# Moving the gate's small tiles to the left side of on-chip memory: all large tiles shift by a fraction of 512 bytes

## The chip, the core and the metric

The kernel runs on one core of a Trainium2 chip. The metric is the device time of one execution in microseconds. Before the change it is 1930.12 us, the median of three runs (1930.12, 1932.39, 1927.75).

## The reference

Three stages follow one another, all in float32:

```python
k_p, v_p = k and v averaged over 8 neighbouring positions
attn = softmax(q @ k_p.T / 8) @ v_p                  # 4 batches, 8 heads, 576 positions
x = attn as [2304, 512]
h = x @ w_in ; x = (h * cos(h)) @ w_out              # 512 -> 2048 -> 512
P = exp(x @ w_gate - max) ; 8 rounds of row and column normalization
out = sum over 8 experts e of P[:, e] * (relu(x @ w1[e]) @ w2[e])   # 512 -> 1024 -> 512
```

The experts are two thirds of the span: each expert's two weight matrices are used in two units of 512 hidden columns, 16 units in all, against three pairs of token blocks (a pair is 768 tokens). That is 48 steps.

## The kernel before, in words

Every float32 operand of a product is split into a high and a low part, and a product is three TensorE matmuls (high by high, high by low, low by high). Each product of a step is computed by Strassen's scheme: seven products of half-size blocks, named P1 to P7.

**One step.** The first layer (`first_layer`, L1057, matmuls on L1077) has the weights `whi`/`wlo` as the stationary operand and the tokens `xc` as the moving operand of 384 columns: 84 matmuls. ScalarE and VectorE apply relu, combine the blocks and split them into `gh`/`gl` (`strassen_result`, L1380). The second layer (`strassen_layer`, L1449, matmuls on L1457) has `gh`/`gl` as the stationary operand and the weights `vhi`/`vlo` as the moving operand of 256 columns: 126 matmuls. In the order of the instructions first-layer matmuls of one step alternate with second-layer matmuls of the step before. The weights come in as `raw` tiles by DMA and are cut into parts by ScalarE, VectorE and GpSimd (`w1_pieces`, L1252, `w2_pieces`, L1288). Tokens are loaded again for every step (`x_loaded`, L1360).

**What sets the order.** The program is a list of nodes (`add`, L169), each with an engine, an estimated duration and the tiles it touches. `schedule` (L263) walks the list with these estimates and writes out each engine's instructions in a fixed order. It asks `place` (L240) whether a tile's slot is free and whether the slot's group is open. It knows slots by name and never by address.

**Where tiles lie.** On-chip memory has a stack on the left, which grows upwards, and one on the right, which grows downwards. Tiles belong to kinds, kinds to pools, pools to groups (L439 to L448). `Group.open` (L88) puts the pools of a group on its stack, one after the other, in the order in which they were named. `base`, `first`, `second` and later `more` are on the left; `early`, then `mid`, `ahead`, `turn` and `late` are on the right. `mid` and what follows it may open when no tile of `early` has any user left. L98 to L100 put a tile `edge` that nothing writes or reads ahead of the pools of `early` and of `mid`; it takes 64 bytes of a partition.

**The addresses.** They follow from the sizes, here in bytes of a partition, and what matters below is what is left of them past a multiple of 512. The left stack starts with a scratch area of 2048, four constants (128), `warm` (64) and `ident` (512): 2752, which is 192 past a multiple of 512. The tokens' slots `xp` (6144 each), the first layer's weights `wp` (2048) and the accumulators (6144) are multiples of 512, so all of them lie at 192. Then come the gate's `wgr` (512), `sel` (64) and `lg` (576). They end 128 further, so whatever follows on the left lies at 320: the raw weights `rawp`, the split activations `gph`/`gpl` and `gbh`/`gbl` (tiles `gh` and `gl`), the second stage's `xq`, `wq`, `tp`, and the accumulators `acx`. The right stack starts at a multiple of 512. Of `early`, the 64 bytes of `edge` put the conversion tiles `cvm`, `cvw`, `cvs` at 448. Of `mid`, `edge` (64), `ones` (512), `pr` (576) and the six scratch tiles `sk` of the gate's normalization (256) make 1408, so that the second layer's weights `wp2` (tiles `vhi` and `vlo`) and all that follow on the right (`xt`, `tmp`, `cps`, `cpc`, `cpt`) lie at 128.

The gate's tiles are made at L1184 to L1190 and used by `logits` (L1195) and `normalization` (L1213). Of `sel` only the first 8 columns are ever used.

Of the kernel before, what the change touches and what calls it, by code (L numbers as in the profile page):

```python
# [23 lines left out]
P = 128  # L24
T = B * S
DM = H * D
KC = DM // P
FU = 512
FC = FU // P
E = 8  # L30
# [3 lines left out]
NT = T // P  # L34
# [6 lines left out]
GW = 32  # L41
# [36 lines left out]
class Group:  # L78
# [9 lines left out]
    def open(self):  # L88
        if self.stack is not None:
            return  # L90
        if self.over:
            self.over.open()
        for g in self.after:
            if not g.closed and g.stack is not None:
                g.stack.close()
            g.closed = True
        self.stack = self.graph.ctx.enter_context(ExitStack())
        if self.name in ("early", "mid"):  # L98
            edge = self.stack.enter_context(self.graph.tc.tile_pool(name="edge" + self.name, bufs=1, side=self.side))
            edge.tile([P, 8], F32, name="edge" + self.name)  # L100
        for pool in self.pools:
            self.pools[pool] = self.stack.enter_context(
                self.graph.tc.tile_pool(name=pool, bufs=1, side=self.side, reuse_waits="tile"))
# [40 lines left out]
class Graph:  # L144
# [18 lines left out]
    def buf(self, kind, shape, dtype, name):  # L163
        return Buf(kind, shape, dtype, name)
# [268 lines left out]
def fused_kernel(ctx: ExitStack, tc: tile.TileContext, qT, kT, vT, v0, k1, v1, wa1, wb1, wa2, wb2, wg, out):  # L433
    nc = tc.nc
    g = Graph(ctx, tc)
# [3 lines left out]
    base = g.group("base")  # L439
    first = g.group("first")  # L440
    second = g.group("second")
    early = g.group("early", "right")
    mid = g.group("mid", "right", (early,))
# [10 lines left out]
    def many(group, pool_name, n, strict=False):  # L454
        return g.kind(group, pool_name, [str(i) for i in range(n)], strict)
# [20 lines left out]
    k_pt = many(early, "ptp", 1)  # L476
    k_ck = {n: g.kind(early, "ck", [n]) for n in ("band", "minus", "kbd0", "kbd1")}
    k_gc = {n: g.kind(mid if n in ("ones", "pr") else base, "gc" + n, [n]) for n in ("ones", "wgr", "sel", "lg", "pr")}
    k_sk = {n: g.kind(mid, "sk", [n]) for n in ("m1", "m2", "nm", "rw", "cs", "cr")}
    k_w2 = many(ahead, "wp2", W2, True)  # L480
    k_wd = g.join(k_cs, k_m, k_cw, strict=True)
    k_wu = g.kind(ahead, "wp2", [str(i) for i in range(10)], True)
# [682 lines left out]
    for u in range(U1):  # L1165
# [16 lines left out]


    gate = {n: buf(k_gc[n], s, F32, n) for n, s in (  # L1184
        ("ones", [P, P]), ("wgr", [P, KC, GW]), ("sel", [P, 2 * E]), ("lg", [P, NT, E]), ("pr", [P, NT, E]))}
    ones, wgr, sel, lg, pr = (gate[n] for n in ("ones", "wgr", "sel", "lg", "pr"))
    add("V", 0.17, lambda: nc.vector.memset(ones.tile, 1.0), [], [ones])
    load(lambda: wgr.tile, lambda: wg, P * KC * GW * 4, writes=[wgr])
# [397 lines left out]
```

## Time and profile before

| | |
|---|---|
| median of three runs | 1930.12 us (1927.75 to 1932.39) |
| the profiled execution's own time | 1929.34 us |
| its span, from the first to the last instruction | 1927.6 us |
| mean granted TensorE clock | 0.999 |
| TensorE, matmuls | 1907.3 us busy, 99% of the span, 13012 matmuls |
| VectorE, ScalarE, GpSimd | 1531.9, 1096.6, 427.4 us busy |
| DMA | 406.79 MB, 211 GB/s over the span |

The profiled execution is 0.8 us under the median. Its own time is 1.7 us longer than its span. A matmul's listed duration overlaps with its neighbours', so the pace of TensorE is read from the starts of matmuls that follow one another, or from the pieces of the chain of waits, which give the time of a row of them.

### The profile page before, as it was taken

The page shows a single profiled execution, that of the slowest core. Times are in us where ns is not written, and L with a number is a line of the kernel's source. Part 1 is how long each engine was busy: PE and PEld are TensorE (multiplying, and loading weights), DVE is VectorE, ACT ScalarE, POOL GpSimd, SP SyncE. Part 2 cuts the span into 40 slices and gives each one's busy share as a digit, 9 for nine tenths or more (in the row PEclk, how much of TensorE's full clock was granted, in tenths as well). Part 3 has the DMA queues.
Part 4 walks back from the last instruction along what each step waited for, and adds up shares of the span by engine and source line. Part 5 has one row for each costly group of instructions (what it writes and reads, how often), then busy time and mean ns, then how long its engine had stood idle before and what let it go on. Part 6 is the DMA issues. An engine that isn't in the chain of part 4 may idle for free.

```text
span 1927.6 us, 34292 instructions
## 1 busy us (share of the span) xinstructions
PE 1907.3 (99%) x13012; PEld 1872.0 (97%) x13012; DVE 1531.9 (79%) x2823; ACT 1096.6 (57%) x2354; POOL 427.4 (22%) x341
## 2 busy tenths in 40 slices
PE   8999999999999999999999999999999999999999
PEld 6789998899999999999999999999999999999998
DVE  8998888987787777777787787777777877877776
ACT  5664445675556666555556565565555565655553
POOL 2523245453202021212112021212121120212120
PEclk9999999999999999999999999999999999999999
DMA  8567564487656546546546455465465464554552
GB/s 294 169 193 236 194 198 138 176 288 239 231 225 229 228 186 237 212 181 236 211 177 262 168 231 229 184 238 210 183 236 211 178 262 170 229 231 180 229 216 113
DMA packets 107478, 406.79 MB, mean 211 GB/s; under 512 B 11825, under 2 KB 16561, under 8 KB 107313
## 3 DMA queue, kind: packets, MB, share of 16 engines
q1 hardware_dynamic: 106768, 403.55, 56.4%
q8 instruction: 102, 1.67, 0.4%
q0 software_dynamic: 544, 1.05, 0.3%
q14 instruction: 64, 0.52, 0.1%
HBM read 363.40 MB, written 41.16 MB: 210 GB/s over the span
## 4 chain that ended last, share of the span: by engine, by line
PE 91%; DVE 5%; ACT 1%; DMA 1%; issue 1%; POOL 0%; SPq 0%; DVEq 0%; POOLq 0%; ACTq 0%
PE pc L1457 21%; PE py L1077 17%; PE qc L1457 16%; PE pv L1077 11%; PE px L1077 11%; PE po L894 3%; PE po L895 3%; PE po L896 3%; PE ph L894 1%; PE ph L896 1%; PE ph L895 1%; PE ptr L803 0%; DVE at L540 0%; DVE cw L858 0%; PE psc L714 0%
## 5 line engine op out<-in xcount | busy, mean ns | idle before, releaser
L1457 PE MATMUL pc<-vhi,gl 128*128 128x256 f32 x1152 | 321.6, 279 | 0.0
L1457 PE MATMUL pc<-vhi,gh 128*128 128x256 f32 x1152 | 321.5, 279 | 0.0
L1457 PE MATMUL pc<-vlo,gh 128*128 128x256 f32 x1152 | 321.3, 279 | 0.0
L1077 PE MATMUL py<-xc,whi 128*128 128x384 f32 x1152 | 293.3, 335 | 0.0
L540 POOL TENSOR_TENSOR raw<-raw 128x512 f32<-128x512 f32 x45 | 59.1, 1314 | 895.4 <-DVE wlo L540 542.1
L540 DVE TENSOR_TENSOR gl<-sf,gh 128x384 fp32r<-128x384 f32 x384 | 228.4, 624 | 30.9 <-ACT gh L523 30.9
L523 ACT ACTIVATE gh<-sf 128x384 fp32r<-128x384 f32 x384 | 195.0, 524 | 92.1 <-DVE sf L540 90.1
L1457 PE MATMUL qc<-vhi,gh 128*128 128x256 f32 x864 | 243.6, 282 | 0.9 <-DVE qc L540 0.5
L1457 PE MATMUL qc<-vhi,gl 128*128 128x256 f32 x864 | 241.6, 280 | 0.0
L1457 PE MATMUL qc<-vlo,gh 128*128 128x256 f32 x864 | 240.8, 279 | 0.0
L1457 PEld LDWEIGHTS pc<-vlo,gh 128*128 128x128 f32 x1152 | 216.6, 188 | 0.0
L1457 PEld LDWEIGHTS pc<-vhi,gl 128*128 128x128 f32 x1152 | 216.3, 188 | 0.0
L1457 PEld LDWEIGHTS pc<-vhi,gh 128*128 128x128 f32 x1152 | 215.5, 187 | 0.1
L1077 PEld LDWEIGHTS py<-xc,whi 128*128 128x128 f32 x1152 | 199.7, 188 | 1.3 <-ACT py L523 0.6
L1077 PE MATMUL px<-xc,whi 128*128 128x384 f32 x768 | 195.8, 335 | 0.0
L1077 PE MATMUL pv<-xc,whi 128*128 128x384 f32 x768 | 195.8, 335 | 0.0
L1077 PE MATMUL py<-xc,wlo 128*128 128x384 f32 x576 | 193.2, 335 | 0.0
L1457 PEld LDWEIGHTS qc<-vhi,gh 128*128 128x128 f32 x864 | 161.8, 187 | 3.4 <-DVE qc L540 1.1
L1457 PEld LDWEIGHTS qc<-vlo,gh 128*128 128x128 f32 x864 | 162.5, 188 | 0.0
L1457 PEld LDWEIGHTS qc<-vhi,gl 128*128 128x128 f32 x864 | 162.3, 188 | 0.0
L1077 PEld LDWEIGHTS pv<-xc,whi 128*128 128x128 f32 x768 | 130.7, 188 | 0.0
L1077 PEld LDWEIGHTS px<-xc,whi 128*128 128x128 f32 x768 | 130.5, 188 | 0.0
(235 smaller groups left out, 4676.1 us busy)
## 6 DMA issues: line engine op xcount, KB each, us to landing
xc<-xc SPq DMA_DIRECT2D x357, 768.0 KB, 6.7
wc<-wac SPq DMA_DIRECT2D x112, 256.0 KB, 3.3
raw<-wa SPq DMA_DIRECT2D x48, 512.0 KB, 4.0
raw<-wb SPq DMA_DIRECT2D x48, 512.0 KB, 7.4
wac<-wc SPq DMA_DIRECT2D x64, 256.0 KB, 3.8
out<-acc SPq DMA_DIRECT2D x18, 256.0 KB, 2.0
qc<-qt SPq DMA_DIRECT2D x30, 128.0 KB, 3.1
wf<-cw SPq DMA_DIRECT2D x12, 256.0 KB, 3.6
```

The lines of the kernel that those rows point to most:

```text
L523: lambda: nc.scalar.activation(out=out(), in_=in_(), func=func, **{k: v() if callable(v) else v for k, v in more.items()}),
L540: (nc.gpsimd if e == "G" else nc.vector).tensor_tensor(out=out(), in0=in0(), in1=in1(), op=op)
L894: nc.tensor.matmul(out=ps, lhsT=lh, rhs=rh, start=(i == 0), stop=False)
L895: nc.tensor.matmul(out=ps, lhsT=lh, rhs=rl, start=False, stop=False)
L896: nc.tensor.matmul(out=ps, lhsT=ll, rhs=rh, start=False, stop=(i == total - 1))
L1077: nc.tensor.matmul(out=ps(), lhsT=l[:, k], rhs=r[:, c, :], start=(start and c + n == 0), stop=(c + n == 3), skip_group_check=True)
L1457: nc.tensor.matmul(out=ps, lhsT=l[:, r], rhs=m[:, k], start=(start and h + n == 0), stop=(h + n == 3), skip_group_check=True)
```

## The change

Three edits, all of them about where tiles lie. `early` has no `edge` tile any more. The six scratch tiles `sk` move from `mid` on the right to `base` on the left. `sel` is declared with 48 columns in place of 16; its use stays the same.

```diff
@@ Group.open
-        if self.name in ("early", "mid"):
+        if self.name == "mid":
             edge = self.stack.enter_context(self.graph.tc.tile_pool(name="edge" + self.name, bufs=1, side=self.side))
             edge.tile([P, 8], F32, name="edge" + self.name)
@@ fused_kernel
-    k_sk = {n: g.kind(mid, "sk", [n]) for n in ("m1", "m2", "nm", "rw", "cs", "cr")}
+    k_sk = {n: g.kind(base, "sk", [n]) for n in ("m1", "m2", "nm", "rw", "cs", "cr")}
@@ fused_kernel, the gate
-        ("ones", [P, P]), ("wgr", [P, KC, GW]), ("sel", [P, 2 * E]), ("lg", [P, NT, E]), ("pr", [P, NT, E]))}
+        ("ones", [P, P]), ("wgr", [P, KC, GW]), ("sel", [P, 6 * E]), ("lg", [P, NT, E]), ("pr", [P, NT, E]))}
```

By the same sums: on the left `wgr`, `sel`, `lg` and `sk` now take 512 + 192 + 576 + 256 = 1536 bytes, three times 512, so what follows lies at 192 and no longer at 320. On the right `edge`, `ones` and `pr` take 1152, so `wp2` and what follows lie at 384 and no longer at 128. The tiles of `early` move up by 64 bytes, `cvm`, `cvw` and `cvs` to a multiple of 512. Tiles of `xp`, `wp` and the first four accumulators stay where they are.

## Rows read from the trace of the kernel before

**Rows 1.** The page, part 1: busy us, share, instructions of each engine.

```profile
PE 1907.3 (99%) x13012; PEld 1872.0 (97%) x13012; DVE 1531.9 (79%) x2823; ACT 1096.6 (57%) x2354; POOL 427.4 (22%) x341
```

**Rows 2.** Stretches of the span: length, each engine's busy us, clock, DMA share, GB/s.

```profile
0.00:100.00 100.00, 90.07 (x554) 73.21 (x555) 89.79 (x176) 62.30 (x133) 40.94 (x51) 1.00 0.73 235
100.00:200.00 100.00, 98.39 (x569) 94.35 (x568) 89.32 (x168) 56.23 (x110) 28.75 (x24) 1.00 0.66 212
200.00:300.00 100.00, 98.56 (x566) 98.35 (x565) 86.44 (x152) 49.63 (x100) 41.31 (x39) 1.00 0.65 207
300.00:400.00 100.00, 97.62 (x618) 88.52 (x617) 86.14 (x149) 61.13 (x110) 44.43 (x35) 1.00 0.46 158
400.00:500.00 100.00, 100.00 (x573) 100.00 (x572) 73.32 (x123) 56.01 (x111) 42.10 (x27) 1.00 0.69 240
500.00:600.00 100.00, 99.61 (x691) 96.55 (x690) 85.45 (x196) 65.14 (x136) 12.00 (x7) 1.00 0.63 242
600.00:1900.00 1300.00, 1300.00 (x9272) 1298.31 (x9271) 1004.53 (x1832) 737.09 (x1634) 217.90 (x159) 1.00 0.55 212
```

**Rows 3.** The chain of waits, 1000 to 1012 us: start, us, what.

```profile
1000.75 1.04 PE py L1077 x6
1001.79 0.70 PE qc L1457 x6
1002.50 2.12 PE pc L1457 x18
1004.61 1.04 PE pv L1077 x6
1005.66 0.70 PE qc L1457 x6
1006.36 0.71 PE pc L1457 x6
```

**Rows 4.** The page, part 5: the two layers' largest groups of matmuls.

```profile
L1457 PE MATMUL pc<-vhi,gl 128*128 128x256 f32 x1152 | 321.6, 279 | 0.0
...
L1077 PE MATMUL py<-xc,whi 128*128 128x384 f32 x1152 | 293.3, 335 | 0.0
...
L1457 PE MATMUL qc<-vhi,gh 128*128 128x256 f32 x864 | 243.6, 282 | 0.9 <-DVE qc L540 0.5
```

**Rows 5.** The chain of waits, 400 to 500 us.

```profile
400.14 2.08 PE py L1077 x12
...
406.95 1.05 PE pv L1077 x6
...
410.62 1.06 PE pv L1077 x6
...
415.90 1.04 PE py L1077 x6
```

**Rows 6.** Instructions in order of time, TensorE, 465.1 to 467.2 us.

```profile
465.10 0.34 PE L894 MATMUL po<-gh,wc 128*128 128x384 f32 x1
...
466.15 0.34 PE L894 MATMUL po<-gw,wc 128*128 128x384 f32 x1
...
467.20 0.34 PE L1077 MATMUL px<-xh,wc 128*128 128x384 f32 x1
```

**Rows 7.** Groups by line, ScalarE, 384 elements: busy us, mean ns, idle before.

```profile
L523 ACT ACTIVATE gh<-spare 128x384 fp32r<-128x384 f32 x96 | 50.1, 522 | 38.1 <-DVE spare L1407 38.0
L523 ACT ACTIVATE gh<-c 128x384 fp32r<-128x384 f32 x96 | 49.8, 519 | 1.5
...
L523 ACT ACTIVATE gh<-r 128x384 fp32r<-128x384 f32 x80 | 39.8, 518 | 22.5 <-PE po L896 11.2 <-DVE r L540 11.1
...
L523 ACT ACTIVATE gw<-r 128x384 fp32r<-128x384 f32 x16 | 8.2, 519 | 1.1 <-DVE r L540 1.1
```

**Rows 8.** Groups by line, VectorE, 512 elements.

```profile
L540 DVE TENSOR_TENSOR wlo<-raw,whi 128x512 fp32r<-128x512 f32 x79 | 53.9, 698 | 14.2 <-ACT whi L523 14.2
...
L540 DVE TENSOR_TENSOR vlo<-raw,vhi 128x512 fp32r<-128x512 f32 x68 | 46.4, 683 | 31.2 <-ACT vhi L523 31.2
```

**Rows 9.** The page, part 6: DMA issues, KB each, us to landing.

```profile
xc<-xc SPq DMA_DIRECT2D x357, 768.0 KB, 6.7
...
raw<-wa SPq DMA_DIRECT2D x48, 512.0 KB, 4.0
raw<-wb SPq DMA_DIRECT2D x48, 512.0 KB, 7.4
```

## The prediction

> **What bounds the kernel now.** I read the busy shares first, then the stretches of the span, then the chain of waits, and last the durations of single groups. The shares name TensorE: 1907.3 of 1927.6 us [rows 1]. A share is an average, so the stretches come next. They show two different parts. Up to 600 us TensorE's busy time falls short of the stretch by 9.93, 1.61, 1.44, 2.38, 0 and 0.39 us, 15.75 us in all, and there attention, weight conversion and DMA share the work. From 600 to 1900 us it is busy 1300.00 of 1300 us while VectorE has 1004.53, ScalarE 737.09 and GpSimd 217.90, all at a granted clock of 1.00 of the 2.4 GHz level [rows 2]. The reader is to see that in these two thirds of the span nothing but TensorE's own pace counts: an operation that gets 10% slower on VectorE, or a load that lands a microsecond later, has room.
>
> The chain of waits gives that pace, because here it consists of matmuls alone. Eighteen second-layer matmuls take 2.12 us, 117.8 ns each; six first-layer matmuls take 1.04 us, 173.3 ns each [rows 3]. A step has 84 in the first layer and 126 in the second, 14.56 + 14.84 = 29.4 us, and 48 steps make 1411 us. So what the kernel does in the experts is 4032 intervals of 173.3 ns and 6048 of 117.8 ns. (The 6048 are 3 x 1152 and 3 x 864, one row of each shown [rows 4].)
>
> **The change part by part.** The three edits add no instruction and remove none: the `edge` tile is never touched, the extra columns of `sel` are never read or written, and `sk` holds the same tiles under the same names. Nothing is moved in any queue, SP's and GpSimd's included. The order of the work is also the same as far as I can follow it by hand: the planner asks only whether a slot is free and its group open. `sk` in `base` is open from the start, where in `mid` it had to wait for `early` to close; but its first user needs all six blocks' logits, which need the last output of the stage before, long after `early` has no users left. So the first part of the sum is **0 us for instructions and order**.
>
> Waits: tiles of `sk` used to lie on memory that the conversion tile `cvm` had held; that wait goes, on work of the stage before, whose output the gate's logits need anyway, 0 us. The tiles of `ahead`, `turn` and `late` now move by 256 bytes against `early`'s 64, and all left tiles by the same 384, so which new tile lies on which old one hardly changes: going through the sizes I find no overlap that is new between `early` and the weights `wp2`, and `wp2`'s third slot no longer touches a tile of `at`. 0 us.
>
> What is left is whether an address alone changes a duration. I take the engines one by one.
>
> *ScalarE.* The same copy of 384 elements takes 522 ns from an input at 192, 519 ns from one at 128 and 518 ns from one at 320, all into a tile at 320, and 519 ns into one at 192 [rows 7]. Four placements, 4 ns apart. 0 us.
>
> *VectorE.* The subtraction with its output and one input at 192 has a mean of 698 ns, that with both at 128 has 683 [rows 8]. The 15 ns may be placement or GpSimd at work beside it. For `vlo`, which moves from 128 to 384, I bound it by 0 and +15 ns: some 112 such operations on either engine, 1.7 us of VectorE time in a stretch where it is idle for 295 us. What covers it is that idle time; without the cover 1.7 us would show. 0 us.
>
> *DMA.* The `raw` loads, 96 of 512 KB, land after 4.0 and 7.4 us [rows 9] in tiles that go from 320 to 192; the token loads `xc` stay where they were. A tenth more on the slower ones would be 0.7 us each, and TensorE waits for none of them after 600 us [rows 2]. 0 us there. Before 600 us the waits are 15.75 us in sum; if a tenth of these hung on placement it would be 1.6 us either way. I keep that as an end, and take 0.
>
> *TensorE.* This is the term that decides. The first layer keeps both addresses (192 and 192): 0 us. The second layer's stationary operand goes from 320 to 192 and its moving operand from 128 to 384. No row has that combination, so I bound it. In the stretch from 400 to 500 us operands lie at 192, 320 and others in many combinations. Twelve matmuls of 384 columns take 2.08 us, and six take 1.04, 1.05 or 1.06 us [rows 5]; in the experts, with everything at 192, six take 1.04 us [rows 3]. The nearest row for the question is a pair side by side: the six matmuls from 465.10 us have a moving operand at 320 (`gh` and `gl`), the six from 466.15 us one at 192 (`gw`), and both sixes take 1.05 us [rows 6]. That says that moving an operand by 128 bytes is worth less than 0.01 us in six, or 2 ns each.
>
> The lower end: if the second layer ran at the first layer's pace per column, 173.3 x 256 / 384 = 115.6 ns, it would gain 2.2 ns on each of 6048, **-13 us**. The upper end: if it lost what the slowest six in the mixed stretch lose against the fastest, 1.06 against 1.04 us or 1.9%, it would take 120.1 ns, 2.3 ns more on each of 6048, **+14 us**. Between them I take 0, by the pair, which is the nearest row.
>
> The Trainium skill has a rule that would make of this much more. Its page "TensorE: Matmul & The Clock Gate", section "Back-to-back issue gap", gives 262 cycles for a warm matmul of 256 columns, 109.2 ns. By that the second layer carries 8.6 ns per matmul that the page does not know, and if placement were their cause and the change ended it, the sum would be an estimated -52 us. The same page, "Step-by-step: what each phase is for", says that stationary and moving operand come through two independent read ports, so that loading one does not slow the other; by that placement cannot be the cause. The trace bears out the second: the excess is there in every placement that it shows.
>
> **The sum.** 0 in each term, against the profiled execution's own time of 1929.34 us, which is 0.8 us under the median of the runs shown. I forecast the median, 1930.1 us.
>
> **The rivals.** *Faster: the old pair of addresses costs the second layer something.* Its excess over a bare 256 columns at 2.4 GHz (106.7 ns) is 11.1 ns, 10.4%; the first layer's over 160 ns is 13.3 ns, 8.3%. So the second layer is the slower of the two per column, and it is the one with operands on two different remainders. If the new pair takes it to the first layer's pace, the time is 1930.1 - 13 = 1917 us; with half of that 1923.5. Against it: a matmul has a fixed part as well as a part per column, and a fixed part weighs more on 256 columns than on 384 whatever the addresses are. Chance 0.25.
>
> *Slower: the new pair of addresses collides where the old one did not.* The place is the same 6048 matmuls, as the weight load of the next one runs while the moving operand streams. It decides from 0.65 ns per matmul on (3.9 us over 6048). With the full price above the time is 1930.1 + 14 = 1944 us. For it speaks that six matmuls in the mixed stretch can take 1.06 us; against it, that the same kind of six (`pv`) takes 1.06 us at one time and 1.05 at another in that stretch, so that its spread need not be one of placement, and that the pair at 465 us shows none. Chance 0.17.
>
> *The waits before 600 us shift.* The conversion tiles and the raw inputs move too, and with them the order in which VectorE and GpSimd meet. It is worth up to 1.6 us by the bound above, 1928.5 to 1931.7, and stays inside no change.
>
> *The change doesn't do what it says.* If a size were rounded otherwise than I take it, all large tiles would lie on some other remainder. By the rows that is the same question with the same two ends, so it has no chance of its own.
>
> **How the numbers follow.** A measurement of this kernel can tell about 0.2% from no change, 3.9 us. No change has the rest, 0.58, and its own range is 1926 to 1934. The 8-in-10 range takes in the half price of the faster case and stops short of its full price, and takes the nearer part of the slower case: 1918 to 1937. That leaves about 0.1 out on either side.
>
> **What would show it.** Right: second-layer pieces of eighteen at 2.12 us, first-layer pieces of six at 1.04 us, TensorE busy for all of 600 to 1900 us, and the same number of matmuls there to within a few. Faster, for the reason given: eighteen in 2.08 us, with the first layer unchanged, and some 85 matmuls more (0.9%) between 600 and 1900 us. Slower: eighteen in 2.16 us. I would be wrong in kind if the first layer's pace changed, whose operands did not move, or if the difference lay before 600 us.

## The result: 1908.0 us in the first runs, 1905.4 in a second set, 21 to 25 us less

The changed kernel takes 1908.03 us, the median of four runs (1904.94 to 1910.66), against 1929.34 (median of four, 1927.75 to 1932.39) for the kernel before: ratio 0.9887, 95% interval 0.9866 to 0.9908. A second set, run i2 below, gives 1905.43 against 1930.62: ratio 0.9870, 0.9855 to 0.9885. The prediction of no change was wrong; the change is faster, by 1.1 to 1.3%, and by more than the forecast range of 1918 to 1937 us allowed.

### The profile page after: what moved, and what is told of

Its sections match the earlier page's. It is cut to its first block, busy times and chain, and to the rows that moved or that the text cites. A ratio compares the mean times of both kernels' runs of the same rounds, so it can differ in the third digit from the quotient of the medians.

```text
span 1909.0 us, 34292 instructions
## 1 busy us (share of the span) xinstructions
PE 1889.6 (99%) x13012; PEld 1851.5 (97%) x13012; DVE 1530.6 (80%) x2823; ACT 1095.1 (57%) x2354; POOL 430.7 (23%) x341
## 3 DMA queue, kind: packets, MB, share of 16 engines
q0 software_dynamic: 544, 1.05, 0.3%
## 4 chain that ended last, share of the span: by engine, by line
PE 92%; DVE 6%; ACT 1%; issue 1%; DMA 1%; SPq 0%; DVEq 0%; ACTq 0%
PE pc L1457 20%; PE py L1077 17%; PE qc L1457 16%; PE px L1077 11%; PE pv L1077 11%; PE po L894 3%; PE po L896 3%; PE po L895 3%; PE ph L894 2%; PE ph L896 2%; PE ph L895 2%; DVE at L540 1%; PE ptr L803 1%; PE px L817 1%; PE psc L714 0%
## 5 line engine op out<-in xcount | busy, mean ns | idle before, releaser
L1457 PE MATMUL pc<-vlo,gh 128*128 128x256 f32 x1152 | 318.0, 276 | 0.0
L1457 PE MATMUL pc<-vhi,gl 128*128 128x256 f32 x1152 | 318.0, 276 | 0.0
L1457 PE MATMUL pc<-vhi,gh 128*128 128x256 f32 x1152 | 318.0, 276 | 0.0
L1457 PE MATMUL qc<-vhi,gh 128*128 128x256 f32 x864 | 241.6, 280 | 1.0 <-DVE qc L540 0.5
L1457 PE MATMUL qc<-vlo,gh 128*128 128x256 f32 x864 | 238.9, 276 | 0.0
L1457 PE MATMUL qc<-vhi,gl 128*128 128x256 f32 x864 | 238.8, 276 | 0.0
L1457 PEld LDWEIGHTS pc<-vhi,gh 128*128 128x128 f32 x1152 | 216.3, 188 | 0.1
L1457 PEld LDWEIGHTS pc<-vhi,gl 128*128 128x128 f32 x1152 | 216.3, 188 | 0.0
L1457 PEld LDWEIGHTS pc<-vlo,gh 128*128 128x128 f32 x1152 | 216.2, 188 | 0.0
L1457 PEld LDWEIGHTS qc<-vhi,gh 128*128 128x128 f32 x864 | 162.2, 188 | 4.8 <-DVE qc L540 1.1
L1457 PEld LDWEIGHTS qc<-vhi,gl 128*128 128x128 f32 x864 | 162.3, 188 | 0.0
L1457 PEld LDWEIGHTS qc<-vlo,gh 128*128 128x128 f32 x864 | 162.1, 188 | 0.0
```

Source lines behind the costliest of these rows:

```text
L1457: nc.tensor.matmul(out=ps, lhsT=l[:, r], rhs=m[:, k], start=(start and h + n == 0), stop=(h + n == 3), skip_group_check=True)
```

## The profile after, read against the rows of before

The page of the changed kernel, part 1 and the largest groups of part 5, which answer to [rows 1] and [rows 4]:

```profile
PE 1889.6 (99%) x13012; PEld 1851.5 (97%) x13012; DVE 1530.6 (80%) x2823; ACT 1095.1 (57%) x2354; POOL 430.7 (23%) x341
...
L1457 PE MATMUL pc<-vhi,gl 128*128 128x256 f32 x1152 | 318.0, 276 | 0.0
...
L1077 PE MATMUL py<-xc,whi 128*128 128x384 f32 x1152 | 293.7, 335 | 0.0
```

The numbers of instructions are the same on every engine, and they stand in the same order. TensorE has lost 17.7 us of busy time, and it was lost in L1457, the second layer: a matmul there lasts 276 ns where it lasted 279. The first layer has kept its 335. VectorE and ScalarE have their old sums within 1.5 us.

The stretches of the changed kernel, with the columns of [rows 2]:

```profile
0.00:100.00 100.00, 90.90 (x523) 72.93 (x523) 84.62 (x172) 58.98 (x128) 35.89 (x48) 0.91 0.69 220
...
600.00:1880.00 1280.00, 1280.00 (x9270) 1277.05 (x9270) 1003.07 (x1835) 736.99 (x1636) 221.78 (x159) 1.00 0.56 215
```

The same stretch of before:

```profile
600.00:1880.00 1280.00, 1280.00 (x9126) 1278.31 (x9125) 991.83 (x1808) 729.67 (x1617) 217.90 (x159) 1.00 0.55 213
```

TensorE is busy for all 1280 us in both, and after the change it gets through 144 more matmuls. At 1280 / 9270 = 138 ns each that is 19.9 us: nearly the whole gain lies in the stretch where, as the prediction said, nothing but TensorE's pace counts. The first 100 us went the other way (523 matmuls against 554); that is no effect of the change and is taken up at the end.

The chain of waits, 1000 to 1012 us, beside [rows 3]:

```profile
1000.08 1.04 PE pv L1077 x6
1001.13 0.68 PE qc L1457 x6
1001.81 0.68 PE pc L1457 x6
...
1003.85 1.05 PE py L1077 x6
...
1010.75 1.36 PE pc L1457 x12
```

Six matmuls of 256 columns take 0.68 us where they took 0.70 or 0.71, and twelve take 1.36: 113.3 ns each where it was 117.8. Six of 384 columns still take 1.04, now and then 1.05. Over all intervals from one start to the next, between 600 and 1850 us, the means are 117.75 before and 113.99 ns after for 256 columns (5340 and 5427 of them), 173.92 and 174.25 for 384 columns. Over the whole experts that is 6048 x -3.76 = -22.7 us and 4032 x +0.33 = +1.3 us, -21.4 us in sum.

## The experiments

In all of them a place is what is left of an address past a multiple of 512, as before. W and X are the places of the first layer's stationary operand (`wp`) and moving operand (`xp`), L and R those of the second layer's (`gh`/`gl`, and `wp2`). d1 = X - W and d2 = R - L are taken modulo 256. Before the change d1 is 0 and d2 is 64 (128 - 320 = -192); after it d1 is 0 and d2 is 192. The letters of the theories are those of the expectations quoted.

Every edit is one of the changed kernel and alters sizes of tiles, by columns that nothing reads: the `edge` tile moves R, the width of `sel` moves L, and an unused pad between `xp` and `wp` moves W and with it what follows. In h3 a wider `warm` moves everything on the left. To make room the scratch area is halved, which moves everything on the left by a multiple of 512. The diffs are shortened to what differs from run to run; the line of the scratch area and the two lines that make a pad's tile stand only where they come first.

One size is to be put right for these sums. In the program as built the `edge` tile takes 32 bytes, and the right stack starts 32 bytes short of a multiple of 512. W, X, L and R lie as stated, before, after and in every run; the tiles of `early` moved from 448 to 480 with the change, and not to a multiple of 512.

### Which of the two moves did it

**e1** moves the stationary operand alone, **e2** the moving operand alone.

```diff
 e1
-            edge.tile([P, 8], F32, name="edge" + self.name)
+            edge.tile([P, 72], F32, name="edge" + self.name)
 e2
-  ("sel", [P, 6 * E])
+  ("sel", [P, 80])
 both
-  dynamic_dma_scratch_size=2048
+  dynamic_dma_scratch_size=1024
```

> Second layer: stationary operand at 192 as after the change, moving operand at 128 as before it (a smaller scratch area makes room and moves nothing by other than a multiple of 512). Theory S, the stationary operand's place alone sets the interval (320 is bad, 192 good): 113.4 ns per second-layer matmul, about 1908 us. Theory M, the moving operand's place alone sets it (128 is bad, 384 good): 118 ns, about 1929 us. Theory D, what counts is the distance between the two (moving minus stationary, modulo 512: 320 before, 192 after, 448 here): either of the two values, and then e2 tells.

> Second layer: stationary operand at 320 as before, moving operand at 384 as after. Theory S: 118 ns, about 1929 us. Theory M: 113.4 ns, about 1908 us. Theory D (distance 64 here): if this and e1 are both fast or both slow, neither operand alone decides, and D or a like rule of the pair holds.

e1 (L 192, R 128) took 1909.3 us, e2 (L 320, R 384) 1927.66, beside 1931.6 for the kernel before. The chain of waits and the stretch of e1:

```profile
999.99 0.68 PE pc L1457 x6
...
600.00:1880.00 1280.00, 1280.00 (x9265) 1277.03 (x9264) 1003.00 (x1832) 735.51 (x1633) 221.42 (x159) 1.00 0.56 215
```

and of e2:

```profile
1000.02 0.70 PE qc L1457 x6
1000.73 2.12 PE pc L1457 x18
...
600.00:1880.00 1280.00, 1280.00 (x9124) 1278.30 (x9123) 993.76 (x1811) 729.70 (x1618) 217.53 (x159) 1.00 0.56 213
```

The stationary operand's move by 128 brings 139 of the 144 matmuls, the moving operand's by 256 nothing (9124 against 9126). A move by 256 changes no distance modulo 256, a move by 128 does; but it could still be the stationary operand's own place.

### Place or distance

**h1** leaves the stationary operand at 320 and moves the other one. **h3** moves both layers' four operands by 64.

```diff
 h1
-            edge.tile([P, 8], F32, name="edge" + self.name)
+            edge.tile([P, 40], F32, name="edge" + self.name)
-  ("sel", [P, 6 * E])
+  ("sel", [P, 80])
 h3
-            edge.tile([P, 8], F32, name="edge" + self.name)
+            edge.tile([P, 120], F32, name="edge" + self.name)
-    warm = const.tile([P, 16], F32, name="warm")
+    warm = const.tile([P, 32], F32, name="warm")
```

> Second layer: stationary back at 320 as before the change, moving operand at 256, so that their distance is 192 modulo 256 as after it; first layer unchanged. Theory Q: 113.4 ns, about 1908 us, though the stationary operand lies where it was slow. Theory S (the stationary operand's own place is bad at 320): 118 ns, about 1929 us.

> All large tiles, left and right, 64 bytes past their places in the changed kernel, so that every distance is as there. Theory Q: 113.4 and 174.2 ns, about 1908 us. If absolute places counted (a tile that crosses a border of 256 or 512 bytes once more or less): another value in either layer.

The stretch of h1 (L 320, R 256, d2 192), and then of h3 (d1 0, d2 192, as after the change):

```profile
600.00:1880.00 1280.00, 1280.00 (x9239) 1277.20 (x9238) 1002.13 (x1830) 734.34 (x1631) 221.18 (x159) 1.00 0.56 215
```

```profile
600.00:1880.00 1280.00, 1280.00 (x9272) 1277.03 (x9271) 1004.29 (x1835) 736.46 (x1636) 222.14 (x159) 1.00 0.56 215
```

h1 took 1911.3 us and h3 1905.7, beside 1928.76. With the stationary operand where it was before the change, h1 gets 113 of the 144 matmuls: the distance counts. What it lacks lies at the start of its rows: the first four intervals of a row of 256 columns have means of 119.7, 121.5, 115.9 and 114.2 ns, and from the fifth on it runs at 113.3 to 113.4. h3 has the changed kernel's pace to 0.1 ns in both layers, with every operand 64 bytes further: a shift of all four together does not count.

### Other distances in the kernel

**e3**, **e4**, **f1** to **f4** and **h2** put the operands at other distances.

```diff
 e3
+            edge.tile([P, 56], F32, name="edge" + self.name)
+  ("sel", [P, 128])
+    base.pools["pad48"] = None
+            if pool.startswith("pad"):
+                self.pools[pool].tile([P, int(pool[3:])], F32, name=pool)
 e4
+            edge.tile([P, 120], F32, name="edge" + self.name)
 f1
+            edge.tile([P, 24], F32, name="edge" + self.name)
+  ("sel", [P, 96])
+    base.pools["pad80"] = None
 f2
+  ("sel", [P, 80])
+    base.pools["pad96"] = None
 f3
-        if self.name == "mid":
+        if self.name == "none":
+  ("sel", [P, 104])
+    base.pools["pad72"] = None
 f4
+            edge.tile([P, 16], F32, name="edge" + self.name)
+  ("sel", [P, 88])
+    base.pools["pad88"] = None
 h2
+  ("sel", [P, 128])
+    base.pools["pad48"] = None
```

> Second layer: both operands at 192 (distance 0); first layer: the stationary weights moved from 192 to 384 against a moving operand at 192 (distance 320, the one that the second layer had before). Theory S: second layer 113.4 ns; first layer slower than 173.3 if 384 is a bad place for it. Theory M: second layer unknown, since 192 was not tried; first layer 173.3 ns. Theory D: first layer slower than 173.3 ns, by about 4.5 ns if a matmul of 384 columns pays the same, which would be 18 us over 4032.

> Second layer: stationary at 192, moving at 448 (distance 256), first layer unchanged. Theory S: 113.4 ns, about 1908 us. Theory M: unknown place, anything from 113.4 to 118 ns. Theory D: an untried distance; a value other than 113.4 ns speaks against S.

> Theory Q: the pace of the second layer is a function of the distance from the stationary to the moving operand modulo 256 (so far 64: 118 ns, 192: 113.5 ns, 0: 119.6 ns). Here the second layer has 128 (192 and 320), an untried value between the two: 113 to 118 ns. The first layer gets 192, the good value of the second (weights at 0, tokens at 192): if it obeys the same rule and is slow at 0 now, it falls from 173.3 to about 170 ns, 13 us over 4032. Theory E, a matmul of 384 columns has room enough for the next weight load at any distance: it stays at 173.3 ns.

> Second layer as after the change (distance 192): 113.4 ns by Q. First layer at distance 128 (weights at 64, tokens at 192): 170 to 178 ns by Q, 173.3 ns by E; with 173.3 the time is that of the changed kernel, about 1908 us.

> Both layers at distance 224 modulo 256, half a step of 64 past the good value: if the rule goes by blocks of 64 bytes, the second layer has a value between those of 192 (113.4 ns) and 0 (119.6 ns); if it goes smoothly, about 116 ns. First layer 173.3 ns by E.

> Both layers at distance 160 modulo 256, half a step short of the good value. Second layer between the values of 128 (f1) and 192 (113.4 ns); below 113.4 ns if the best place lies there. First layer 173.3 ns by E.

> Second layer as after the change (192 and 384), first layer at distance 64 (weights at 384, tokens at 192), which in e3 ran at 173.6 ns on the mean against 174.2 in the changed kernel. Theory Q: second layer 113.4 ns, first 173.6 ns, some 2 us under the changed kernel's 1908. Theory H: the second layer's pace depends on how the first layer leaves it, as f2 suggests, and can be anything from 113.4 to 118 ns.

Mean intervals by layer (600 to 1850 us), matmuls between 600 and 1880 us, the time of the run and of the kernel before beside it. e1, e3, f3, f4 and h2, single executions, hold a stretch of lower clock in their first 50 us that is told of at the end and costs some 3 to 5 us; f2 has two short ones (3.4 us each) before 110 us, and the kernel before beside e1 to e4 has a mean clock of 0.997. So the times are good to some 5 us; the intervals and the counts are free of it.

| run | d1 | d2 | 384 col., ns | 256 col., ns | matmuls | us | before |
|---|---|---|---|---|---|---|---|
| before | 0 | 64 | 173.92 | 117.75 | 9126 | | |
| after | 0 | 192 | 174.25 | 113.99 | 9270 | 1908.03 | 1929.34 |
| h1 | 0 | 192 | 173.79 | 115.08 | 9239 | 1911.3 | 1928.76 |
| e4 | 0 | 0 | 174.06 | 119.26 | 9069 | 1935.6 | 1931.6 |
| e3 | 64 | 0 | 173.67 | 120.37 | 9036 | 1945.26 | 1931.6 |
| f1 | 192 | 128 | 174.98 | 119.26 | 9044 | 1941.44 | 1929.85 |
| f2 | 128 | 192 | 175.99 | 116.09 | 9139 | 1930.48 | 1929.85 |
| f3 | 224 | 224 | 174.93 | 118.49 | 9076 | 1942.19 | 1929.85 |
| f4 | 160 | 160 | 174.64 | 117.97 | 9104 | 1938.39 | 1929.85 |
| h2 | 64 | 192 | 174.37 | 117.83 | 9115 | 1933.2 | 1928.76 |

Theory S falls with e3 and e4: L is at 192, and they are slower than before. D's slower first layer did not come in e3 (173.67 ns). For 256 columns 0 is among the worst distances, 192 the best. But d2 = 192 alone is not enough, and with that theory Q misses in f2 and h2 (113.4 ns expected); it also misses in f1, with 119.26 ns outside 113 to 118, and 174.98 in the first layer in place of 170. f2 and h2 have the second layer's operands at the very places of the changed kernel (L 192, R 384) and X too (192); only W differs, 64 and 384 in place of 192. They are hardly better than before. The chain of f2 shows both paces side by side:

```profile
1000.56 1.36 PE pc L1460 x12
...
1004.03 0.68 PE qc L1460 x6
1004.71 2.04 PE pc L1460 x18
...
1008.51 0.71 PE pc L1460 x6
1009.22 0.71 PE qc L1460 x6
```

Matmuls of one kind, at the same places, take 113.3 ns in one row and 118 in the next. So at d2 = 192 there are two paces, and which one a row gets depends on how it is entered: between 600 and 1850 us, the 42 rows of twelve that begin with `pc` after six `py` all go at the slow one, and the 70 rows that begin with `pc` after twelve matmuls of 384 columns all go at the fast one. That is where the first layer's places come in, though its own pace hardly varies.

### The matmuls by themselves

**g1** holds rows of 36 matmuls on one core with nothing beside them: four places of the stationary operand (sa to sd, 64 bytes apart) by four of the moving one (xa to xd), 256 columns (n) and 384 (m), in one order (u) and in the reverse (v). The model's work is left out, and the output is zeros.

```diff
+    def row(name, n, s, m, count):
+        acc = bank(name)
+        for k in range(count):
+            a, b = 16 * s + 128 * (k % 6), 16 * m + 256 * (k % 3)
+            nc.tensor.matmul(out=acc[:, :n], lhsT=w[:, a:a + 128], rhs=x[:, b:b + n], start=(k == 0), stop=(k == count - 1))
```

> Matmuls alone: all of the model's work is left out and the output is zeros. Rows of 36 matmuls of 256 and of 384 columns, with the stationary and the moving operand each at four places 64 bytes apart (a, b, c, d), all sixteen pairs, in two orders (u forwards, v backwards); no other engine works. Theory Q (the distance between the operands modulo 256 sets the pace): for 256 columns about 113.5 ns where the distance is 192, 118 where it is 64, 119 to 120 at 0 and 128, the same in each of the four pairs of one distance and in both orders; for 384 columns 173.3 at 0 and 64, 175 to 176 at 128 and 192. Theory C (the pace comes from other engines' accesses that collide with TensorE's): all sixteen the same. Theory H (a row keeps the phase in which it was entered): values of one pair differ between the two orders.

The chain of waits of g1, one row of matmuls a line (start, us, what):

```profile
32.05 4.31 PE unsaxa L43 x36
36.36 4.24 PE unsaxb L43 x36
40.60 4.27 PE unsaxc L43 x36
44.88 4.09 PE unsaxd L43 x36
48.97 4.24 PE unsbxa L43 x36
...
106.25 6.24 PE umsaxb L43 x36
112.48 6.33 PE umsaxc L43 x36
...
247.31 4.10 PE vnsbxa L43 x36
251.41 4.24 PE vnsaxd L43 x36
...
264.16 4.33 PE vnsaxa L43 x36
```

Divided by 36, 256 columns take 119.4 to 120.3 ns at distance 0, 117.8 at 64, 118.3 to 118.9 at 128, and 113.6 to 114.2 or 117.8 at 192. All 16 pairs fall on these by their distance alone. From 32 us on no other engine is at work here and transfers are down to 1 GB/s, so the pace does not come from their accesses (the expectations' theory C falls). `sa`/`xd` and `sb`/`xa` both have distance 192: the first takes 4.09 us in one order and 4.24 in the other, the second the reverse. A row at this distance settles within its first half dozen matmuls and keeps to one pace for the rest of its 36, and which one depends on what ran before it: theory H. At 384 columns the range over these pairs is small, 6.24 to 6.37 us, 173.3 to 176.9 ns.

**g2** steps the distance by 16 bytes (a to p) and, in rows r, s and t, narrows the stationary operand to 96, 64 and 32 columns. Each row is entered from twelve matmuls at a fixed distance (`resetu`: 0). Again matmuls alone, with zeros as output.

```diff
-            a, b = 16 * s + 128 * (k % 6), 16 * m + 256 * (k % 3)
+            a, b = 128 * (k % 6), 4 * m + 256 * (k % 3)
-  lhsT=w[:, a:a + 128]
+  lhsT=w[:, a:a + cols]
```

> Matmuls alone, the model's work left out, output zeros. The moving operand 0, 16, 32 ... 240 bytes past the stationary one modulo 256 (a to p), rows of 30, each entered from 12 at distance 0 (u) or at 128 (v), for 256 and 384 columns; then stationary operands of 96, 64 and 32 columns at distances 0, 64, 128, 192. Theory W (what collides is the next matmul's weight load with the running matmul's moving operand): the narrower the stationary operand, the less each distance costs, and with 32 columns all four distances agree within 1 ns, near 256 columns' own 106.7 ns plus a few. Theory X (the moving operand's reads collide among themselves or with PSUM writes; the distance only stands for the moving operand's place): narrow stationary operands leave the values of 113 to 120 ns as they are. For the finer steps: if banks are as wide as the steps of 64, the values between lie between their neighbours; a value under 113 ns anywhere would be a better place for the second layer.

The chain of waits of g2, rows of 30: distances 96 (g), 112 (h), 128 (i) and 192 (m), then 32 columns at 0 (a) and 192 (m).

```profile
63.67 3.60 PE ung L43 x30
...
68.70 3.46 PE unh L43 x30
...
73.60 3.56 PE uni L43 x30
...
93.56 3.42 PE unm L43 x30
...
467.54 3.53 PE tna L43 x30
...
482.23 3.41 PE tnm L43 x30
```

The means of the intervals, without the first six of a row, never go below 113.3 ns, and 192 is a narrow place: 16 bytes to either side of it the rows take 119.4 and 119.2 ns, while 112 gives 114.5 between 120 and 118.8. At 384 columns the worst distance is 240, with 180.1 ns. With narrower stationary operands the distances that reach 113.5 ns are others (64 at 96 columns, 0 at 64; 64, 128 and 192 at 32), and one at 32 columns still takes 117.7. The width of the stationary operand matters, then, but neither of the theories is borne out as it was put. What exactly meets inside TensorE's reads stays open.

**g3** runs the kernel's own alternation, rows of six at 384 columns and of twelve and six at 256, for all 64 combinations of three distances in steps of 64 from W: X, L and R, named by letters (`aad`: X - W = 0, L - W = 0, R - W = 192). Matmuls alone, zeros as output.

```diff
+    def steps(first, second, name):
+        for what in "aa0a0a0a1" * 2:
+            if what == "a":
+                row(f"f{name}", 384, *first, 6)
+            else:
+                row(f"g{name}", 256, *second, 12 if what == "0" else 6)
```

> Matmuls alone, the model's work left out, output zeros. Sixes of 384 columns and twelves of 256 alternate as in the experts; the first layer's stationary operand at a, its moving operand and the second layer's two at all 64 combinations of four places. Theory H (the good state of distance 192 is entered from some phases and not from others): with the first layer at distance 0 the second layer has 113 to 115 ns at each of the four pairs of distance 192, with the first at 64 about 118, as in h2. The least sum of both layers names the best version to try: by the kernels so far the one of the change (first 0, second 192), at about 174.2 and 113.9 ns.

The chain of waits of g3 for `aad`, the places after the change, and `acd`, those before it:

```profile
95.12 1.36 PE gaad L42 x12
96.48 1.04 PE faad L42 x6
97.52 1.36 PE gaad L42 x12
...
268.14 1.41 PE gacd L42 x12
269.55 1.04 PE facd L42 x6
270.60 1.41 PE gacd L42 x12
```

With the kernel's 4032 and 6048 intervals the means make 4032 x 174.73 + 6048 x 113.26 = 1389.5 us for `aad`, and 4032 x 173.97 + 6048 x 117.30 = 1410.8 for `acd`. The difference, 21.3 us, is what the intervals of the two kernels gave, 21.4. For the others it gives, relative to `acd`, e3 +18.0, f1 +9.6, e4 +9.4, f2 +4.7, h2 +3.5 and h1 -13.1 us; the kernel's own intervals, from the table above, give +14.8, +13.4, +9.7, -1.7, +2.3 and -16.7. So the matmuls alone, in the kernel's alternation, tell what the kernel does to within some 6 us.

The distances within the two layers do not settle it. `aba` has 0 and 192 like `aad`, only with L and R moved by 64 against W, and takes 117.80 ns where `aad` takes 113.26. Theory H expected 113 to 115 at all four such pairs: two of the four came so (the others have 115.40 and 117.80). It expected about 118 with the first layer at 64, where `bcb` has 114.95 and `bdc` 116.87. So the distance between the layers' operands counts too, and which combination a row enters well was found by trying, not by a rule.

### The best combination, in the kernel

g3's best is `dad` (W 0, X 192, L 0, R 192), 1388.4 us, 1.1 under the change's. **i1** puts the kernel there; **i2** is the changed kernel again, with no edit, beside it.

```diff
 i1
-            edge.tile([P, 8], F32, name="edge" + self.name)
+            edge.tile([P, 56], F32, name="edge" + self.name)
+    base.pools["pad80"] = None
```

> First layer's weights W at 0, its moving operand X at 192 (distance 192, moving less stationary, modulo 256), second layer's stationary operand L at 0 like W, its moving operand R at 192 (distance 192): the combination that was best with matmuls alone. Theory H (pace by distance, with a state that a row of matmuls keeps from where it was entered): 173.6 ns in the first layer and 113.8 in the second, so 4032 x 173.62 + 6048 x 113.82 = 1388.4 us against 1389.5 us for the changed kernel's places: about 1 us under it, 1907, between 1904 and 1912. Rival: the state entered differs with the real order of the rows, as it can for a distance of 192 in the first layer: then 176.7 ns there, 4032 x 2.0 = 8 us more, about 1916.

> The changed kernel again, on the same chip, beside the run above: 1908, between 1904 and 1912, with 113.5 ns in the second layer and 174.2 in the first. Theory H and its rival expect the same here.

i1 took 1903.73 us (1902.33 to 1907.09), ratio 0.9867, 0.9850 to 0.9883; i2 1905.43 (1904.80 to 1906.28), ratio 0.9870, 0.9855 to 0.9885. The chain and stretch of i1:

```profile
1002.53 0.68 PE qc L1460 x6
1003.22 1.04 PE py L1080 x6
1004.25 1.36 PE pc L1460 x12
...
600.00:1880.00 1280.00, 1280.00 (x9287) 1276.94 (x9286) 1005.99 (x1839) 737.75 (x1642) 221.56 (x159) 1.00 0.56 214
```

The first 600 us of the kernel before, and then both stretches of i2:

```profile
0.00:600.00 600.00, 584.25 (x3561) 550.98 (x3562) 510.46 (x959) 350.44 (x699) 209.54 (x182) 1.00 0.64 216
```

```profile
0.00:600.00 600.00, 585.05 (x3592) 551.91 (x3593) 511.18 (x960) 352.10 (x702) 208.37 (x182) 1.00 0.64 217
600.00:1880.00 1280.00, 1280.00 (x9268) 1277.03 (x9267) 1004.04 (x1836) 736.71 (x1637) 221.15 (x159) 1.00 0.56 214
```

The rival's 176.7 ns in the first layer did not come; its mean is 173.04 (174.26 in i2), the second layer's 114.40 (114.03). That makes 6048 x 0.37 - 4032 x 1.22 = -2.7 us, and the 19 matmuls more are 2.6 us. The medians differ by 1.7 us, less than their intervals tell apart: i1 is as good as the change, perhaps a little better.

i2's first 600 us hold 3592 matmuls against 3561 before. Of the 24.4 us between the profiles of before and of i2, 142 matmuls more in the stretch shown make 19.6, so some 5 us lie outside it, nearly all in these 31. The stage ahead of the experts has matmuls of 384 columns on operands that moved too: those of `po` (L894 to L896) have mean intervals from start to start of 175.53 ns before and 173.87 in i2, those of `ph` 174.35 and 173.14, which is some 2.8 us over 1152 and 772 of them. The other 2 us were not taken apart.

## Why the prediction was wrong, point by point

*Instructions, order, waits, ScalarE, VectorE, DMA: 0 each.* Right for the experts. Order and numbers are unchanged, TensorE waits for nothing after 600 us, `raw` from `wb` lands after 7.7 us against 7.4 [rows 9], and TensorE does not wait for it. Before 600 us the sum held only the waits, 1.6 us at most, and no term for the pace of the second stage's matmuls; some 5 us came from there in i2, of which 2.8 are that pace.

*TensorE: "Between them I take 0, by the pair, which is the nearest row."* This is the step that failed. The pair [rows 6], like the mixed stretch [rows 5], consists of matmuls of 384 columns. g1 shows that these vary by 2% over its pairs of places, 173.3 to 176.9 ns, while those of 256 columns vary by 6%, 113.6 to 120.3. The question was one of 256 columns, and the trace of before held a single pair of places for it. The row looked nearest by place, but was far by shape. Nor did the pair hold the rest still. It was read by the moving operand's place, and by e2, h1 and h3 it is distances that count. The stationary tiles `wc` lie at 192 (`wp`) or at 320 (`wq`), and by the program's addresses each of the two sixes has four matmuls at distance 0 and two at 128: the pair compared the same distances with each other, so its 1.05 us twice could not show what a distance costs.

*The ends, -13 and +14 us.* The lower end took the first layer's pace per column for the best the second could reach. It was no floor: 113.3 ns for 256 columns is 0.443 ns a column, 173.3 for 384 is 0.451. The interval term measured -22.7 us and not -13. The upper end was about right: e3 and e4 put the second layer at 120.37 and 119.26 ns, where the prediction had 120.1. The slower rival was a real possibility, one choice of sizes away.

*The rival "Faster: the old pair of addresses costs the second layer something".* Its mechanism is what happened; its price was too small by 8 us by the first set, and its chance was 0.25. What was held against it, that a fixed part weighs more on 256 columns whatever the addresses, fell with the 0.68 us of six. Its signs came, and stronger: twelve in 1.36 us are eighteen in 2.04 and not 2.08, and there were 144 matmuls more from 600 to 1880 us, not 85 to 1900.

*"Wrong in kind if the first layer's pace changed, whose operands did not move".* It did change, by 0.33 ns (174.25 against 173.92), and the change sits where a row begins: the second interval of a 384-column row has a mean of 178.9 ns after and 174.4 before, while from the seventh on both run at 173.3 to 173.4. That is small. It looks like the same carrying over that spoils f2 and h2; no run was made for it alone.

*The read ports.* Rows of g1, with no other engine of the core at work, change their pace by 6% with the distance of their two operands. The Trainium skill ("TensorE: Matmul & The Clock Gate", "Step-by-step: what each phase is for") has the two operands come through independent read ports, so that a weight load takes nothing from the running matmul; the prediction concluded that placement cannot be the cause, and that the trace bore this out. By e1 and g1 that conclusion is wrong: the pace goes by where the two operands lie to each other, and the measurement decides. What meets in between no run here shows. The same page's "Back-to-back issue gap" gives 262 cycles for 256 columns. The best row here, 113.3 ns, is 272 cycles of 2.4 GHz; of the 8.6 ns over the page's figure the change ended 4.5, and none of the places tried ended the rest.

## What to carry to other kernels

In a kernel like this one, where float32 matmuls with a weight load each bound the time, the operands' places are a parameter like any other: try the distances of moving and stationary operand modulo 256 bytes, those between alternating layers included, by padding a tile nobody reads. Look for it with matmuls alone, but in the kernel's own alternation of shapes, since the pace of a row can depend on the row before it, and then measure the kernel. And when a row of the trace is to bound an unknown, it should be near in shape before it is near in place, and what it holds still should be looked up on both operands.

## What the runs showed that was not expected

**Two paces at one distance.** At 192, a row of 256 columns runs at 113.3 or 117.8 ns a matmul once it has settled, and keeps to it for as long as it lasts (g1: 36 matmuls). Which of the two it is depends on the row before it.

**The clock, early in some runs.** A piece of the chain of waits of the changed kernel's first profile, and its stretches:

```profile
22.34 6.65 PE pk L678 x40
...
24.00:26.00 2.00, 2.00 (x17) 1.83 (x16) 1.93 (x5) 0.85 (x2) 0.00 (x0) 1.00 0.97 315
26.00:27.00 1.00, 1.00 (x7) 0.87 (x6) 1.00 (x3) 0.47 (x1) 0.00 (x0) 0.75 1.00 342
27.00:28.00 1.00, 1.00 (x7) 1.00 (x6) 1.00 (x3) 0.00 (x0) 0.00 (x0) 0.50 0.98 358
...
38.00:40.00 2.00, 1.77 (x8) 1.28 (x8) 1.70 (x4) 0.88 (x2) 0.00 (x0) 0.50 0.92 267
40.00:41.00 1.00, 1.00 (x8) 1.00 (x8) 0.49 (x3) 1.00 (x3) 0.00 (x0) 0.92 0.28 98
```

The granted clock fell from 1.00 to 0.50, the 1.2 GHz level, while TensorE was busy without a gap in a row of forty matmuls, and came back at 40 us. i2, the same kernel, had 1.00 throughout the first 100 us. The profile with the fall has 523 matmuls in the first 100 us, i2's has 554: some 5 us. The four first runs order themselves by it: 1904.94 and 1906.52 us at mean clocks of 1.000 and 0.999, 1909.53 and 1910.66 at 0.995. Of the seven runs of the kernel before beside i2, three are at 0.997 and four at 0.999 or 1.000, the four with a median of 1929.98 us. Against i2's four, all at 0.999, like with like, the change is worth some 24.5 us. Why the clock falls in one execution and not in the next was not tried.
